# A fused recurrence, tanh feed-forward and top-1 mixture of experts on one core: where the routing's small steps stand in the queues of ScalarE, POOL, SP and PE

## The chip, the cores and the metric

The kernel runs on one core of one Trainium2 chip. The metric is the device time of one execution in microseconds. A profiled execution additionally gives the span from the first to the last instruction and a record of every instruction on the five engines and the DMA queues.

## The reference

Three stages follow one another: a linear recurrence with per-head decay (4 batches, 8 heads, 768 steps, head size 48), a feed-forward layer with `h - tanh(h)`, and a mixture of 8 experts in which each token goes to the one expert with the largest cosine similarity.

```python
# stage 1, per step t
cur = einsum('bhd,bhe->bhde', u[None] * kt, vt)
y[:, :, t] = einsum('bhd,bhde->bhe', rt, state + cur)
state = w[None, :, :, None] * state + einsum('bhd,bhe->bhde', kt, vt)
# stage 2, x is [3072, 384]
h = x @ w_in                     # [384, 2048]
x = (h - np.tanh(h)) @ w_out     # [2048, 384]
# stage 3
xn = x / (norm(x) + 1e-06);  en = expert_emb / (norm(expert_emb) + 1e-06)
logits = xn @ en.T / tau
expert_idx = np.argmax(logits, axis=1)
probs = exp(logits - max);  probs /= probs.sum(-1) + 1e-09
gate_w = probs[arange(N), expert_idx]
for e in range(8):
    out[expert_idx == e] = gate_w * (maximum(x @ w1[e], 0) @ w2[e])   # 384 -> 1024 -> 384
```

## The kernel before, in words

The 3072 tokens are worked in 8 blocks of 3 tiles of 128 tokens. Every product of float32 numbers is made of three products on PE: both operands are split into a rounded half (`hi`) and a remainder (`lo`), and hi·hi, hi·lo, lo·hi are summed in PSUM.

**A block's feed-forward** has 16 steps. A step is `ffn1` (L529 to L536): nine products of 128x384 into one PSUM bank `ph`; then `squares` and `small_tanh` (L574, L583), which make the values on ScalarE (`z` L581, `q` L582, `ghi` L592, a mask L594) and VectorE (L590, L591, `glo` L597); and, three steps later, `ffn2` (L541): nine products that add the step to three accumulators `acc`, one per token tile. The recurrence of the next block is spread between the steps (`pa`, `py`, `am`, L407 to L446). The first six steps of block 0 and the sixteen of block 1 run first, then the other ten of block 0, then blocks 2 to 7, so block 1 is the first to be finished and block 7 the last.

**After a block**, `finish` (L617 to L687) is a generator in four pieces, taken up one at a time. Piece 1 stores the block's rows `xr` to the DRAM table `xs`, takes the logits `l` and the sums of squares `ssq`. Piece 2 finds each token's expert as a one-hot `oh` on VectorE and counts tokens with nine small products on PE into `pk` (L649 to L654). Piece 3 makes each token's row number `irow` on VectorE and lets POOL scatter the token numbers into the DRAM table `tab`, in three indirect DMAs (L666). Piece 4 makes the gate: a root on POOL (`rn`, L673), some small VectorE operations, the exponential `ex` on ScalarE (L678), its sum `se`, and three stores of the gate `gw` by SP into the last columns of `xs` (L686).

**The experts** come after the last block, each with up to 3 tiles of 128 tokens and, for the first ones, a smaller further tile. `places` (L771) loads a list `gts` of token numbers from `tab`, and `rows` (L779) gathers the rows named there from `xs` by indirect DMAs on POOL (L759). The gathered tiles are `rkv` (three per expert), `ktab` and `u_bc`. `columns` (L828) turns a tile on PE (`pt`, L833) and copies it on ScalarE and VectorE to `xt` or `xn`. `load_expert` (L791) loads an expert's weights in four pieces of 768 KB through two staging tiles `eraw` (SP, L799 and L802), each split by ScalarE and VectorE (L810, L811). `wide` (L844) runs the three tiles through 8 steps of `ffn1` (PE L534), `relu` (L610) and `ffn2`; `narrow` (L897) runs a single tile in another arrangement (L904, `hh` L907, L910).

The first expert is chosen while the last block is still computing, so its weights, lists and three tiles are there when the block ends, and its steps 0 to 6 follow at once. What cannot be known before the last block's counts is its fourth tile (`ktab`), and the second expert's list and tiles (`rkv` three times, `u_bc`). At the end of the program's block loop, in this order:

```python
    while pend:
        ffn2_next()
    next(fin)
    next(fin)
    places(0, TB, TB + 1)
    places(1, 0, TB + (KOV > 1))
    for _ in fin:
        pass
    order_rest()
```

What sets the order of work on each engine is a scheduler: the program is written once, the scheduler simulates it with a timeline of its own and puts each engine's instructions into a fixed queue. `with tc.issue_after(x)` adds that what stands inside is placed after the instruction `x`. On the chip every queue is run strictly in order, and an instruction that waits holds up all behind it.

Of the kernel before, what the change touches and what calls it, by code (L numbers as in the profile page):

```python
# [8 lines left out]
F32 = mybir.dt.float32  # L9
# [4 lines left out]
AF = mybir.ActivationFunctionType  # L14
ALU = mybir.AluOpType
# [14 lines left out]
def rwkv__then__tanh_ffn__then__top1_moe_kernel(  # L30
# [14 lines left out]
    nc = tc.nc  # L45
    B = 4
    H, D = w.shape
    NT, DM = out.shape
# [3 lines left out]
    P = 128  # L52
# [475 lines left out]
    def ffn1(lhs, rhs, nk, n, idle=0):  # L528

        ph = ps.tile([P, n], F32, tag="p", name="ph")  # L530
        fill(ph, idle)
        for kk in range(nk):
            for p, (a, b) in enumerate(((0, 0), (0, 1), (1, 0))):
                nc.tensor.matmul(out=ph, lhsT=lhs[a][:, kk, :], rhs=rhs(b, kk),  # L534
                                 start=(kk == 0 and p == 0), stop=(kk == nk - 1 and p == 2))
        return ph  # L536

    def columns_of(xt):
# [46 lines left out]
    def small_tanh(ph, parts, step, between=iter(())):  # L585

        z, q = parts
        ghi = work.tile([P, TOK], F32R, name="ghi", bufs=LAG + 1)
        glo = work.tile([P, TOK], F32R, name="glo", bufs=LAG + 1)
        nc.vector.tensor_tensor(out=ph, in0=ph, in1=z, op=ALU.mult)  # L590
        nc.vector.scalar_tensor_tensor(out=ph, in0=q, scalar=KC, in1=ph, op0=ALU.add, op1=ALU.mult)  # L591
        nc.scalar.activation(out=ghi, in_=ph, func=AF.Copy)  # L592
        mk = work.tile([P, TOK], BF16, name="mk", bufs=1)
        nc.scalar.activation(out=mk, in_=z, func=AF.Relu, bias=lz_t, accum_out=zx[:, step:step + 1])  # L594
        for _ in range(3):
            next(between, None)
        mark["glo"] = nc.vector.tensor_tensor(out=glo, in0=ph, in1=ghi.bitcast(F32), op=ALU.subtract).ins  # L597
        return ghi, glo
# [17 lines left out]
    def finish(j, acc, part=None):  # L616
        l = work.tile([P, TB, E], F32, name="l")  # L617
        ssq = work.tile([P, TB], F32, name="ssq")
        gw = work.tile([P, TB, 2], F32, name="gw")
        for t in range(TB):  # L620
            if part is not None:
                x = part[:, t, :]
                nc.vector.tensor_tensor(out=x, in0=acc[t], in1=x, op=ALU.add)
                acc[t] = x
            nc.vector.tensor_scalar(out=l[:, t, :], in0=acc[t][:, DM:], scalar1=rtau, scalar2=None, op0=ALU.mult)
        for t in range(TB):
            if part is not None:
                xr = part[:, t, :DM]
            else:
                xr = work.tile([P, DM], F32, name="xr")  # L630
                nc.scalar.activation(out=xr, in_=acc[t][:, :DM], func=AF.Copy)
            n = TB * j + t
            nc.sync.dma_start(out=xs[n * P:n * P + P, :DM], in_=xr)
            junk = work.tile([P, TOK], F32, name="t", bufs=1)
            nc.scalar.activation(out=junk, in_=xr, func=AF.Square, accum_out=ssq[:, t:t + 1])
        yield
        bc = [P, TB, E]
        mx = work.tile([P, TB], F32, name="mx")
        nc.vector.tensor_reduce(out=mx, in_=l, op=ALU.max, axis=AX.X)
        nc.vector.tensor_tensor(out=l, in0=l, in1=mx[:, :, None].to_broadcast(bc), op=ALU.subtract)  # L640
        ix = work.tile(bc, F32, name="ix")
        nc.vector.scalar_tensor_tensor(out=ix, in0=l, scalar=0.0, in1=iom[:, None, :].to_broadcast(bc),
                                       op0=ALU.is_ge, op1=ALU.mult)
        nc.vector.tensor_reduce(out=mx, in_=ix, op=ALU.min, axis=AX.X)
        oh = work.tile(bc, BF16, name="oh")
        nc.vector.tensor_tensor(out=oh, in0=iom[:, None, :].to_broadcast(bc),
                                in1=mx[:, :, None].to_broadcast(bc), op=ALU.is_equal)
        pk = ps.tile([P, TB + 1, E], F32, tag="p", name="pk")
        nc.tensor.matmul(out=pk[:, 0, :], lhsT=tri16, rhs=oh[:, 0, :], start=True, stop=True)  # L649
        for t in range(1, TB + 1):  # L650
            if t < TB:
                nc.tensor.matmul(out=pk[:, t, :], lhsT=tri16, rhs=oh[:, t, :], start=True, stop=False)
            for s in range(t):
                nc.tensor.matmul(out=pk[:, t, :], lhsT=ones16, rhs=oh[:, s, :],  # L654
                                 start=(t == TB and s == 0), stop=(s == t - 1))
        yield
        pos = work.tile(bc, F32, name="pos")
        nc.vector.tensor_tensor(out=pos, in0=pk[:, 0:TB, :], in1=cntb[:, None, :].to_broadcast(bc), op=ALU.add)
        nc.vector.tensor_tensor(out=pos, in0=pos, in1=oh, op=ALU.mult)
        row = work.tile([P, TB], F32, name="row")  # L660
        nc.vector.tensor_reduce(out=row, in_=pos, op=ALU.add, axis=AX.X)
        irow = work.tile([P, TB], I32, name="irow")
        nc.vector.tensor_copy(out=irow, in_=row)
        nc.vector.tensor_tensor(out=cntb, in0=cntb, in1=pk[:, TB, :], op=ALU.add)
        for t in range(TB):
            apart("tab", nc.gpsimd.indirect_dma_start(  # L666
                out=tab, out_offset=bass.IndirectOffsetOnAxis(ap=irow[:, t:t + 1], axis=0),
                in_=tokid[:, TB * j + t, :], in_offset=None))
        yield

        rn = work.tile([P, TB], F32, name="rn")
        nc.vector.tensor_scalar(out=rn, in0=ssq, scalar1=1e-30, scalar2=None, op0=ALU.max)
        nc.gpsimd.tensor_tensor(out=rn, in0=rn, in1=half, op=ALU.pow)  # L673
        nc.vector.tensor_scalar(out=rn, in0=rn, scalar1=1e-6, scalar2=None, op0=ALU.add)
        nc.vector.reciprocal(out=rn, in_=rn)
        nc.vector.tensor_tensor(out=l, in0=l, in1=rn[:, :, None].to_broadcast(bc), op=ALU.mult)
        ex = work.tile(bc, F32, name="ex")
        nc.scalar.activation(out=ex, in_=l, func=AF.Exp)  # L678
        se = work.tile([P, TB], F32, name="se")
        nc.vector.tensor_reduce(out=se, in_=ex, op=ALU.add, axis=AX.X)  # L680
        nc.vector.tensor_scalar(out=se, in0=se, scalar1=1e-9, scalar2=None, op0=ALU.add)
        nc.vector.reciprocal(out=se, in_=se)
        nc.vector.tensor_copy(out=gw, in_=se[:, :, None].to_broadcast([P, TB, 2]))
        for t in range(TB):
            n = TB * j + t
            nc.sync.dma_start(out=xs[n * P:n * P + P, DM:], in_=gw[:, t, :])  # L686
        yield  # L687


# [80 lines left out]

    def places(jb, t0, t1):  # L771

        with tc.issue_after(lastg) if jb > 1 else ExitStack():
            eng = nc.gpsimd if jb > 1 else nc.sync
            row = eng.value_load(sxi[0:1, jb, 0:1], min_val=0, max_val=(E - 1) * REG)
            eng.dma_start(out=gts[:, jb, t0:t1],
                          in_=tab[bass.ds(row + t0 * P, (t1 - t0) * P), :].rearrange("(t p) b -> p t b", p=P))

    def rows(jb, t0, t1, n):  # L779
        nonlocal lastg  # L780
# [8 lines left out]
    def load_expert(jb, m, gate, engs=(nc.vector,)):  # L789
# [5 lines left out]
        n = WN // 4  # L795
        for c in range(4):
            t = work.tile([P, n], F32, name="eraw", tag=f"stg{c % 2}", bufs=1)
            if c < 2:
                nc.sync.dma_start(out=t.rearrange("p (k f) -> p k f", k=NK),  # L799
                                  in_=w1e[:, c * 512:(c + 1) * 512].rearrange("(k p) f -> p k f", p=P))  # L800
            else:
                nc.sync.dma_start(out=t.rearrange("p (f d) -> p f d", d=DM),  # L802
                                  in_=w2e.rearrange("(f p) d -> p f d", p=P)[:, 4 * (c - 2):4 * (c - 2) + 4, :])
            m = n // 2
            for s in range(2):
                a = slice(s * m, (s + 1) * m)
                with ExitStack() as es:
                    for g in gate.values():
                        es.enter_context(tc.issue_after(g))
                    nc.scalar.activation(out=hi[c][:, a], in_=t[:, a], func=AF.Copy)  # L810
                    engs[s % len(engs)].tensor_tensor(out=lo[c][:, a], in0=t[:, a], in1=hi[c][:, a].bitcast(F32),  # L811
                                                      op=ALU.subtract)
            yield
# [578 lines left out]
            pass  # L1392
    while pend:
        ffn2_next()
    next(fin)
    next(fin)
    places(0, TB, TB + 1)
    places(1, 0, TB + (KOV > 1))
    for _ in fin:
        pass  # L1400
    order_rest()

    sl = sl + rows(0, TB, TB + 1, NT)
# [73 lines left out]
```

## Time and profile before

| | |
|---|---|
| time, 3 runs | 811.16, 812.74, 815.42 us, median 812.74 us |
| profiled execution | 813.03 us, span 811.4 us |
| PE busy | 778.0 us, 96% of the span, 5938 products |
| VectorE, ScalarE, POOL busy | 506.7, 452.0, 284.1 us |
| mean granted clock of PE | 0.98 |

The granted clock is a share of full speed: 1.00 is 2.4 GHz and 0.50 is 1.2 GHz. A matmul's duration runs to its modelled end, so consecutive ones overlap: nine products of 128x384 take about 1.74 us by their rows. In a timeline, "[4.66 <-DVE l L676]" says that the engine was idle for 4.66 us before the row, until VectorE's instruction of line 676 wrote `l`. Times are microseconds from the span's start.

### The profile page before, as it was taken

The numbers are of one execution on the slowest core, as the hardware profiler recorded it, in microseconds if no ns is written. First come the engines' busy times: TensorE is split into PE (matmuls) and PEld (weight loads), VectorE is DVE, ScalarE is ACT, GpSimd is POOL, SyncE is SP. The second block draws the span as 40 slices with busy tenths as digits, with TensorE's granted clock in tenths as the row PEclk, the third lists the DMA queues.
The fourth block names the chain that finished last, engine by engine and source line by source line (L and its number), as shares of the span: only waits on it lengthen the run. The fifth ranks groups of instructions, "written<-read, shape, count | busy, mean of one in ns | idle before, by whom it ended". The sixth has DMA issues, their size and how long they took to land. (4 is left out here: it accounts for less than half of the span.)

```text
span 811.4 us, 15572 instructions
## 1 busy us (share of the span) xinstructions
PE 778.0 (96%) x5938; PEld 729.3 (90%) x5938; DVE 506.7 (62%) x1080; ACT 452.0 (56%) x1044; POOL 284.1 (35%) x296
## 2 busy tenths in 40 slices
PE   8899999999999999999999999999899999999992
PEld 5679898889999999999999999999789999999992
DVE  7977974766765866875865865686544435554510
ACT  5676686547456556566566567684443444454421
POOL 3721640563550750750741610333340313331111
PEclk9899999999999999999999999999999999999997
DMA  8834350223330240331231210331733445554300
GB/s 275 284 89 134 111 194 1 85 83 122 106 114 23 67 155 21 83 125 43 86 116 54 86 45 15 120 96 31 229 102 118 137 129 166 175 171 143 111 28 30
DMA packets 41861, 87.33 MB, mean 108 GB/s; under 512 B 9744, under 2 KB 21440, under 8 KB 40754
## 3 DMA queue, kind: packets, MB, share of 16 engines
q1 hardware_dynamic: 37042, 76.74, 29.1%
q0 software_dynamic: 4320, 9.51, 3.6%
q8 instruction: 48, 0.79, 0.4%
q14 instruction: 35, 0.29, 0.2%
q10 hardware_dynamic: 416, 0.00, 0.0%
HBM read 67.46 MB, written 19.47 MB: 107 GB/s over the span
## 5 line engine op out<-in xcount | busy, mean ns | idle before, releaser
L534 PE MATMUL ph<-xt,wq 128*128 128x384 f32 (+2 forms) x1712 | 343.4, 343 | 2.2 <-ACT wt L284 1.4
L534 PEld LDWEIGHTS ph<-xt,wq 128*128 128x128 f32 x1712 | 304.2, 190 | 7.8 <-issue 1.7
L545 PE MATMUL acc<-wq,ghi 128*128 128x392 f32 (+2 forms) x1120 | 289.9, 344 | 0.9 <-ACT ghi L610 0.5
L545 PEld LDWEIGHTS acc<-wq,ghi 128*128 128x128 f32 (+1 forms) x1120 | 200.8, 187 | 6.5 <-issue 1.2
L545 PE MATMUL acc<-wq,glo 128*128 128x392 f32 (+2 forms) x560 | 185.6, 342 | 0.0
L581 ACT ACTIVATE z<-ph 128x384 f32<-128x384 f32 x128 | 62.6, 489 | 89.1 <-PE ph L534 88.6
L545 PEld LDWEIGHTS acc<-wq,glo 128*128 128x128 f32 (+1 forms) x560 | 104.3, 187 | 1.3 <-DVE glo L597 0.3
L592 ACT ACTIVATE ghi<-ph 128x384 fp32r<-128x384 f32 x128 | 62.7, 490 | 67.7 <-DVE ph L591 62.9
L590 DVE TENSOR_TENSOR ph<-ph,z 128x384 f32<-128x384 f32 x128 | 71.8, 561 | 45.2 <-ACT z L581 44.8
L597 DVE TENSOR_TENSOR glo<-ph,ghi 128x384 fp32r<-128x384 f32 x128 | 70.9, 554 | 40.9 <-ACT ghi L592 39.7
L764 POOL DMA_INDIRECT out_dram<-ob,gts x27 | 28.7, 1063 | 156.2 <-ACT ob L842 150.7
L582 ACT ACTIVATE q<-z,sb_t 128x384 f32<-128x384 f32 x128 | 78.9, 617 | 3.7
L591 DVE SCALAR_TENSOR_TENSOR ph<-q,ph 128x384 f32<-128x384 f32 x128 | 71.7, 560 | 12.0 <-ACT q L582 3.3
L611 DVE SCALAR_TENSOR_TENSOR glo<-ph,ghi 128x384 fp32r<-128x384 f32 (+2 forms) x56 | 31.4, 563 | 75.5 <-ACT ghi L610 59.8
L594 ACT ACTIVATE mk<-z,lz_t 128x384 bf16<-128x384 f32 x128 | 77.1, 602 | 0.0
L610 ACT ACTIVATE ghi<-ph 128x384 fp32r<-128x384 f32 (+2 forms) x56 | 27.7, 496 | 73.6 <-PE ph L534 72.5
L811 DVE TENSOR_TENSOR wq<-eraw,wq 128x768 fp32r<-128x768 f32 x60 | 58.2, 1008 | 16.0 <-ACT wq L810 11.9
L810 ACT ACTIVATE wq<-eraw 128x768 fp32r<-128x768 f32 x64 | 50.5, 838 | 10.4 <-DMA eraw<-in_moe_w_dram 10.3
L267 POOL TENSOR_TENSOR wq<-wraw,wq 128x768 fp32r<-128x768 f32 (+1 forms) x17 | 30.8, 1810 | 62.6 <-ACT wq L266 62.6
L380 POOL TENSOR_TENSOR rk<-rkv 128x384 f32<-128x384 f32 x18 | 18.4, 1020 | 90.2 <-DMA xs<-xr 42.4
L395 POOL TENSOR_TENSOR am<-ident,cd 128x512 f32<-128x512 f32 x36 | 37.3, 1059 | 11.2 <-DVE cd L385 10.5
L346 POOL TENSOR_TENSOR tt<-tt,tab_k 112x512 f32<-112x512 f32 x20 | 33.2, 1660 | 21.8 <-DMA tt<-in_cols_dram 20.6
(282 smaller groups left out, 886.8 us busy)
## 6 DMA issues: line engine op xcount, KB each, us to landing
eraw<-in_moe_w_dram SPq DMA_DIRECT2D x32, 768.0 KB, 4.9
rkv<-in_rows_dram SPq DMA_DIRECT2D x18, 640.0 KB
tt<-in_cols_dram SPq DMA_DIRECT2D x22, 448.0 KB, 4.0
xd<-xt SPq DMA_DIRECT2D x8, 1152.0 KB, 8.4
wraw<-in_moe_w_in_dram SPq DMA_DIRECT2D x8, 768.0 KB
wraw<-in_moe_w_out_dram SPq DMA_DIRECT2D x8, 768.0 KB, 7.1
xs<-xr SPq DMA_DIRECT2D x21, 192.0 KB, 2.1
rkv<-in_rows_dram SPq DMA_DIRECT2D x4, 256.0 KB, 10.4
```

The lines of the kernel that those rows point to most:

```text
L395: nc.gpsimd.tensor_tensor(out=a, in0=ident[:, None, :].to_broadcast([P, HP, P]), in1=self.cd[:, :, g:g + 1].to_broadcast([P, HP, P]), op=A ...
L534: nc.tensor.matmul(out=ph, lhsT=lhs[a][:, kk, :], rhs=rhs(b, kk), start=(kk == 0 and p == 0), stop=(kk == nk - 1 and p == 2))
L545: mm = nc.tensor.matmul(out=acc[t], lhsT=g[a][:, t * P:t * P + m], rhs=rhs(b, i), start=(i == span[0] and p == 0), stop=(i == span[1] - 1 ...
L581: nc.scalar.activation(out=z, in_=ph, func=AF.Square)
L582: nc.scalar.activation(out=q, in_=z, func=AF.Square, scale=SS, bias=sb_t)
L590: nc.vector.tensor_tensor(out=ph, in0=ph, in1=z, op=ALU.mult)
L591: nc.vector.scalar_tensor_tensor(out=ph, in0=q, scalar=KC, in1=ph, op0=ALU.add, op1=ALU.mult)
L592: nc.scalar.activation(out=ghi, in_=ph, func=AF.Copy)
L594: nc.scalar.activation(out=mk, in_=z, func=AF.Relu, bias=lz_t, accum_out=zx[:, step:step + 1])
L597: mark["glo"] = nc.vector.tensor_tensor(out=glo, in0=ph, in1=ghi.bitcast(F32), op=ALU.subtract).ins
L810: nc.scalar.activation(out=hi[c][:, a], in_=t[:, a], func=AF.Copy)
L811: engs[s % len(engs)].tensor_tensor(out=lo[c][:, a], in0=t[:, a], in1=hi[c][:, a].bitcast(F32), op=ALU.subtract)
```

## The change

Four edits. First, `small_tanh` notes its `ghi` in `mark`, and in all blocks but the last the exponential is placed after the most recent one. Second, in the last block the root moves from piece 4 to piece 3, between the first and the second of POOL's three scatters. Third, at the program's end all of `finish` is taken up before `places`, the places of the first two experts are placed after the last gate's store, and the second expert's weights after its list. Fourth, in the last block the counts are placed after the last product of `ffn1`.

```diff
@@ ffn1
-                nc.tensor.matmul(out=ph, lhsT=lhs[a][:, kk, :], rhs=rhs(b, kk),
-                                 start=(kk == 0 and p == 0), stop=(kk == nk - 1 and p == 2))
+                mark["ph"] = nc.tensor.matmul(out=ph, lhsT=lhs[a][:, kk, :], rhs=rhs(b, kk),
+                                              start=(kk == 0 and p == 0), stop=(kk == nk - 1 and p == 2)).ins
@@ small_tanh
-        nc.scalar.activation(out=ghi, in_=ph, func=AF.Copy)
+        mark["ghi"] = nc.scalar.activation(out=ghi, in_=ph, func=AF.Copy).ins
@@ finish
-        nc.tensor.matmul(out=pk[:, 0, :], lhsT=tri16, rhs=oh[:, 0, :], start=True, stop=True)
+        with tc.issue_after(mark["ph"]) if j == NB - 1 else ExitStack():
+            nc.tensor.matmul(out=pk[:, 0, :], lhsT=tri16, rhs=oh[:, 0, :], start=True, stop=True)
...
+        rn = work.tile([P, TB], F32, name="rn")
+        def norms():
+            nc.vector.tensor_scalar(out=rn, in0=ssq, scalar1=1e-30, scalar2=None, op0=ALU.max)
+            return nc.gpsimd.tensor_tensor(out=rn, in0=rn, in1=half, op=ALU.pow).ins
+        root = None
         for t in range(TB):
-            apart("tab", nc.gpsimd.indirect_dma_start(
-                out=tab, out_offset=bass.IndirectOffsetOnAxis(ap=irow[:, t:t + 1], axis=0),
-                in_=tokid[:, TB * j + t, :], in_offset=None))
+            with tc.issue_after(root) if root else ExitStack():
+                apart("tab", nc.gpsimd.indirect_dma_start(
+                    out=tab, out_offset=bass.IndirectOffsetOnAxis(ap=irow[:, t:t + 1], axis=0),
+                    in_=tokid[:, TB * j + t, :], in_offset=None))
+            if j == NB - 1 and t == 0:
+                root = norms()
         yield
-        rn = work.tile([P, TB], F32, name="rn")
-        nc.vector.tensor_scalar(out=rn, in0=ssq, scalar1=1e-30, scalar2=None, op0=ALU.max)
-        nc.gpsimd.tensor_tensor(out=rn, in0=rn, in1=half, op=ALU.pow)
+        if j < NB - 1:
+            norms()
...
-        nc.scalar.activation(out=ex, in_=l, func=AF.Exp)
+        with tc.issue_after(mark["ghi"]) if j < NB - 1 else ExitStack():
+            nc.scalar.activation(out=ex, in_=l, func=AF.Exp)
...
-            nc.sync.dma_start(out=xs[n * P:n * P + P, DM:], in_=gw[:, t, :])
+            mark["gw"] = nc.sync.dma_start(out=xs[n * P:n * P + P, DM:], in_=gw[:, t, :]).ins
@@ places
-        with tc.issue_after(lastg) if jb > 1 else ExitStack():
+        with tc.issue_after(lastg) if jb > 1 else tc.issue_after(mark["gw"]):
...
-            eng.dma_start(out=gts[:, jb, t0:t1],
+            mark["gts"] = eng.dma_start(out=gts[:, jb, t0:t1], in_=tab[bass.ds(row + t0 * P, (t1 - t0) * P), :]
...
@@ load_expert, around the loads of a piece
+            with tc.issue_after(mark["gts"]) if jb == 1 else ExitStack():
...
@@ the end of the block loop
-    next(fin)
-    next(fin)
+    for _ in fin:
+        pass
     places(0, TB, TB + 1)
     places(1, 0, TB + (KOV > 1))
-    for _ in fin:
-        pass
     order_rest()
```

Since the scheduler writes the queues, three places of them are shown, before and now. The lines of the changed program are higher by up to 16.

The first is ScalarE's queue where block 1 is finished, among the steps of block 0: `z`, `q`, `mk` and `ghi` are one step's values. Before:

```order
L592 ACTIVATE ghi<-ph 128x384
L678 ACTIVATE ex<-l 128x24
L581 ACTIVATE z<-ph 128x384
L582 ACTIVATE q<-z,sb_t 128x384
L594 ACTIVATE mk,zx<-z,lz_t 128x384
```

And with the change:

```order
L592 ACTIVATE ghi<-ph 128x384
L581 ACTIVATE z<-ph 128x384
L582 ACTIVATE q<-z,sb_t 128x384
L594 ACTIVATE mk,zx<-z,lz_t 128x384
L592 ACTIVATE ghi<-ph 128x384
...
L592 ACTIVATE ghi<-ph 128x384
L692 ACTIVATE ex<-l 128x24
```

The exponential, which stood ahead of the next step's values, now stands behind those of two steps. In the later blocks it moves behind one or two `ghi`; in the last block it stood behind the `ghi` (L610) of the first expert's step 3 and now stands ahead of it.

The second is SP's queue at the end of the last block: `xr` and `gw` are stores into `xs`, `gts` the loads of the two lists, `eraw` the second expert's weights; a TENSOR_LOAD reads a number from memory into a register of SP. Before:

```order
L633 DMA xs<-xr 128x384 x3
L791 TENSOR_LOAD sxi
L791 ISA x2
L776 ISA
L776 DMA gts<-tab 128x2
L776 ISA
L776 DMA gts<-tab 128x4x2
L799 ISA
L799 DMA eraw<-in_moe_w_dram 128x3x512
...
L686 DMA xs<-gw 128x2 x3
```

And with the change:

```order
L633 DMA xs<-xr 128x384 x3
...
L700 DMA xs<-gw 128x2 x3
L789 TENSOR_LOAD sxi
L789 ISA x2
L790 ISA
L790 DMA gts<-tab 128x2
L789 TENSOR_LOAD sxi
...
L790 DMA gts<-tab 128x4x2
L815 ISA
L815 DMA eraw<-in_moe_w_dram 128x3x512
```

The three stores of gates moved from behind the lists and two pieces of weights to ahead of them, and a register is now read between the stores and the first list and between the lists.

The third is PE's queue in the first expert: `acc_7109` to `acc_7111` are its three accumulators, `wq_1378` and `wq_1379` the halves of the last weights, and `pt` the turned tiles that hang on the gathers. Before:

```order
L545 MATMUL acc_7109<-wq_1378,glo 128x384
L545 MATMUL acc_7110<-wq_1378,glo 128x384
L545 MATMUL acc_7111<-wq_1378,glo 128x384
L833 MATMUL pt<-ident,ktab 128x128 x3
L833 MATMUL pt<-ident,rkv_119 128x128 x9
L833 MATMUL pt<-ident,u_bc 128x64 x3
L534 MATMUL ph<-xt,wq_72 128x384 x2
```

And with the change:

```order
L545 MATMUL acc_7111<-wq_1378,glo 128x384
L849 MATMUL pt<-ident,ktab 128x128 x3
L545 MATMUL acc_7109<-wq_1378,ghi 128x384
...
L545 MATMUL acc_7109<-wq_1379,ghi 128x384
L849 MATMUL pt<-ident,rkv_119 128x128 x3
L545 MATMUL acc_7110<-wq_1378,ghi 128x384
L849 MATMUL pt<-ident,rkv_119 128x128 x3
```

The scheduler has moved the turned tiles forward: `ktab`'s now stands behind step 4 of `ffn2`, and those of the second expert among the products of step 6; before, all stood behind step 6. The nine counts (`pk`) stand in the same place of PE's queue as before: behind `ffn1` of the first expert's step 0 and the last block's last products, ahead of the first expert's step 1.

## Rows read from the trace of the kernel before

**Rows 1.** Waits of PE over the span: for what; us in total, times, longest
```profile
PE py L438 <- DVE am L412: 2.6, 1, 2.6
PE pt L833 <- DMA rkv<-xs,gts: 1.9, 1, 1.9
...
PE pk L649 <- DVE oh L646: 1.5, 1, 1.5
...
PE pt L833 <- DMA ktab<-xs,gts: 1.0, 1, 1.0
PE pt L910 <- issue: 0.7, 1, 0.7
...
PE acc L545 <- ACT ghi L610: 0.5, 1, 0.5
```

**Rows 2.** Windows: us, busy of PE, PEld, DVE, ACT, POOL; granted clock, DMA share, GB/s
```profile
164.00:168.00 4.00, 4.00 (x15) 3.73 (x14) 2.10 (x5) 1.97 (x5) 2.05 (x4) 0.58 0.09 3
585.00:589.00 4.00, 3.65 (x14) 3.22 (x13) 1.68 (x7) 0.82 (x2) 0.00 (x0) 0.50 0.36 133
589.00:594.00 5.00, 5.00 (x22) 4.33 (x21) 2.39 (x3) 2.86 (x5) 0.00 (x0) 0.77 0.13 15
```

**Rows 3.** Timeline of ScalarE, block 1's finish: start us, us, engine, line, operation, idle before
```profile
161.46 0.22 ACT L678 ACTIVATE ex<-l 128x24 f32<-128x24 f32 x1 [4.66 <-DVE l L676]
```

**Rows 4.** Timeline of VectorE, block 1's finish
```profile
160.33 1.10 DVE L676 TENSOR_TENSOR l<-l,rn 128x24 f32<-128x24 f32 x1
...
162.10 0.57 DVE L590 TENSOR_TENSOR ph<-ph,z 128x384 f32<-128x384 f32 x1
...
162.66 0.70 DVE L412 COPY_PREDICATED am<-cmask,pa 128x512 f32<-128x512 uint8 x1
```

**Rows 5.** Timeline of PE, last block and first expert
```profile
542.28 1.15 PE L833 MATMUL pt<-ident,rkv 128*128 128x128 f32 x9
...
572.45 1.74 PE L534 MATMUL ph<-xt,wq 128*128 128x384 f32 x9
...
586.17 3.25 PE L534 MATMUL ph<-xt,wq 128*128 128x384 f32 x9
```

**Rows 6.** Timeline of SP's DMA queue, last block and first expert
```profile
520.21 0.42 SPq L776 DMA_DIRECT2D gts<-tab  x1
...
565.76 0.94 SPq L776 DMA_DIRECT2D gts<-tab  x2
566.97 1.02 SPq L799 DMA_DIRECT2D eraw<-in_moe_w_dram  x2
569.20 1.35 SPq L686 DMA_DIRECT2D xs<-gw  x3
574.93 2.48 SPq L802 DMA_DIRECT2D eraw<-in_moe_w_dram  x2
```

**Rows 7.** Timeline of POOL, last block and first expert
```profile
523.96 1.06 POOL L759 DMA_INDIRECT rkv<-xs,gts  x1 [6.69 <-issue]
...
562.14 0.96 POOL L666 DMA_INDIRECT tab<-tokid,irow  x1 [0.30 <-issue]
563.13 0.92 POOL L673 TENSOR_TENSOR rn<-rn,half 128x3 f32<-128x3 f32 x1
...
575.74 1.33 POOL L759 DMA_INDIRECT ktab<-xs,gts  x1 [11.32 <-issue]
...
581.35 1.00 POOL L759 DMA_INDIRECT u_bc<-xs,gts  x1 [0.31 <-issue]
```

**Rows 8.** Line L686 alone, all 24 stores of gates: the row on landing
```profile
DMA to landing us min/median/max: 1.4/1.5/5.2
```

**Rows 9.** Timeline of ScalarE, first expert
```profile
574.27 1.59 ACT L810 ACTIVATE wq<-eraw 128x768 fp32r<-128x768 f32 x2 [0.49 <-DMA eraw<-in_moe_w_dram]
...
579.66 1.58 ACT L810 ACTIVATE wq<-eraw 128x768 fp32r<-128x768 f32 x2 [3.04 <-DMA eraw<-in_moe_w_dram]
```

**Rows 10.** Timeline of VectorE, last block
```profile
566.52 0.16 DVE L683 COPY gw<-se 128x6 f32<-128x6 f32 x1
```

More of the change, by code (lines that the diff above doesn't have):

```diff
@@ L771, in places @@
     def places(jb, t0, t1):
-        with tc.issue_after(lastg) if jb > 1 else ExitStack():
+        with tc.issue_after(lastg) if jb > 1 else tc.issue_after(mark["gw"]):
             eng = nc.gpsimd if jb > 1 else nc.sync
             row = eng.value_load(sxi[0:1, jb, 0:1], min_val=0, max_val=(E - 1) * REG)
-            eng.dma_start(out=gts[:, jb, t0:t1],
-                          in_=tab[bass.ds(row + t0 * P, (t1 - t0) * P), :].rearrange("(t p) b -> p t b", p=P))
+            mark["gts"] = eng.dma_start(out=gts[:, jb, t0:t1], in_=tab[bass.ds(row + t0 * P, (t1 - t0) * P), :]
+                                        .rearrange("(t p) b -> p t b", p=P)).ins
     def rows(jb, t0, t1, n):
@@ L797, in load_expert @@
             t = work.tile([P, n], F32, name="eraw", tag=f"stg{c % 2}", bufs=1)
[L798 to L803, printed above, removed]
+            with tc.issue_after(mark["gts"]) if jb == 1 else ExitStack():
+                if c < 2:
+                    nc.sync.dma_start(out=t.rearrange("p (k f) -> p k f", k=NK),
+                                      in_=w1e[:, c * 512:(c + 1) * 512].rearrange("(k p) f -> p k f", p=P))
+                else:
+                    nc.sync.dma_start(out=t.rearrange("p (f d) -> p f d", d=DM),
+                                      in_=w2e.rearrange("(f p) d -> p f d", p=P)[:, 4 * (c - 2):4 * (c - 2) + 4, :])
             m = n // 2
```

## The prediction

> **What bounds the kernel now.** PE does nearly all of the span, so I read its waits first. Apart from the start-up there are two places where it waits for something that the change touches. One wait of 2.6 us, for VectorE's `am`, is where block 1 is finished. The others lie together at the first expert: 0.5 for a `ghi`, 1.0 for the gathered `ktab`, 1.9 for the gathered `rkv`, 0.7 in the fourth tile's path, 4.1 us in all; 1.5 us for `oh` stands a little ahead of them [rows 1]. Second, the windows: behind both places PE's granted clock is low, 0.58 over 164 to 168 and 0.50 and 0.77 over 585 to 589 and 589 to 594 [rows 2]. Low is the level of 1.2 GHz, and each time it came behind PE's idle time. One step's nine products took 1.74 us ahead of it and 3.25 in it [rows 5]. Third, the queues, for what ended the waits.
>
> At the first expert the chain goes back to one order in SP's queue. The second expert's weights were issued at 566.97, the gates' stores behind them at 569.20 [rows 6]. A store of gates takes a median of 1.5 us to land, the slowest 5.2 [rows 8]. POOL's first gather waited 11.32 us and started at 575.74, the last of the five ended at 582.35 [rows 7]: that fits stores held up behind 1.5 MB on the same queue, which the gathers need because they read the gate's columns.
>
> **The change part by part.**
>
> *The exponential behind `ghi`.* Where block 1 is finished ScalarE sat 4.66 us before `ex` with the next step's `z` behind it [rows 3]. Now `z` goes first. What is late next is VectorE: its `l` ends at 160.33 + 1.10 = 161.43, and the step's product (L590) and then `am`'s copy follow in its queue. The product ran at 162.10 and the copy at 162.66 [rows 4], 0.56 apart, so the copy can start at about 161.95, 0.7 sooner, and with the two small gate steps gone from between them perhaps 0.8. The bounds are 0 (VectorE meets POOL's transfers anyway) and all of the 2.6 us with its low clock, (1 - 0.58) x 4.0 = 1.7, so 4.3. I take 0.8, because VectorE's own chain is in the rows and stays; the idle time of some 2 us left is nearer to the 2.6 that brought the clock down than to nothing.
>
> In blocks 0 and 2 to 6 no wait of PE hangs on `ex`: 0. The gates there are stored one or two steps later; only the gathers read them. The nearest is block 6, ahead of the first expert's gathers at 523.96 [rows 7], whose tiles PE turns at 542.28 [rows 5]. A delay of two steps is some 6 us against 18; if that cover were gone, PE would wait for the rest. VectorE's `se` now waits for `ex` directly behind a `ghi`, for which `glo` waits too: 0.
>
> *The counts behind nine products.* In PE's queue they stand where they stood, because the last `ffn1` before them was already ahead. The 1.5 us for `oh` stays, and what is behind it (step 1's products) waits as before: 0.
>
> *The root between the scatters.* On POOL the root (0.92 us) goes ahead of two scatters of 0.96 and their 0.3 us gaps [rows 7]: it comes 2.5 us sooner, and the last scatter ends some 1.0 us later, at 564.1. The gate was ready at 566.68 [rows 10], 2.6 us behind the root's end. Now the root ends near 561.5 and the gate comes at 564 to 565, with `ex` no longer behind a `ghi` that waits for step 3.
>
> *SP's queue.* Three stores of gates take 1.35 us to issue [rows 6], until 566.4 at the latest, and land 1.5 later, by 568. The lists wait for the scatters: the first went out at 565.76, 2.7 us behind the last scatter's end [rows 6, 7], so now at 566.8. Behind them the weights: a register read costs about 0.6 us (two lie in the 1.2 us between 567.99 and 569.20), so the weights go out at 568.0 to 568.3 instead of 566.97, 1.2 us later.
>
> *The gathers.* In the last block the first gather started 3.75 us behind the list's issue (520.21 to 523.96) [rows 6, 7]. From 566.8 that gives 570.5. The five took 6.6 us, so the last is issued by 577.1, 5.2 us sooner than before. `ktab` was turned by PE at 580.86 [rows 5], 3.8 us behind its gather's end at 577.07. So it lands at 575.6, the others 1.3 us apart until 580.4.
>
> By the Trainium skill ("DMA: Bandwidth & Descriptors", Anatomy of one DMA) a POOL transfer takes about 2.0 us plus its bytes over 436 GB/s, here an estimate of 2.5 us for the 198 KB of 128 rows. The row's 3.8 is beside two pieces of weights and decides; by the page's figure the gathers land 1.3 us sooner and the time would be about 806.
>
> *PE.* Step 6's nine products began at 572.45 and took 1.74 [rows 5]; step 4's nine of `ffn2` behind them take as long, so PE reaches `ktab`'s tile at about 575.9, and with the products now between the tiles the last one at about 580.2. The gathers are there just in time. Step 5's `ghi` stands ahead of the weights' copies now, so its 0.5 goes. Not all goes: the weights' second pair is issued when the first pair's copies are done, so it too is 1 to 2 us later. Its first copy waited 3.04 us for a transfer issued 4.7 us before [rows 6, 9], and behind it on ScalarE stand the last tiles, step 7's `ghi` and, behind the other copy, `hh`. I leave 1.5 us of waits for that. With 1.5 us in pieces, as at `oh` where the next products ran at full clock, the clock should stay up. The low clock cost 3.65 x 0.50 + 5.00 x 0.23 = 3.0 us [rows 2]. So this place gives 4.1 + 3.0 - 1.5 = 5.6. The bounds are 0 (the waits only move) and 7.1. From there on PE is the bound, and the gain stays to the end.
>
> The sum, against the profiled execution's 813.03 us (span 811.4 and 1.6 around it; 0.3 above the median of the three runs): 813.0 - 0.8 - 5.6 = **806.6 us**.
>
> **The rivals.**
>
> *The gathers come no sooner than the weights (0.21).* The first pair was issued at 566.97 and its second copy began at 574.27, having waited for it [rows 6, 9]: 7.3 us. From 568.0 that is 575.3, and the gathers' traffic comes on top. If each gather is signalled only when what was issued before it has landed, `ktab` comes at 577.5 or later and the last tile at 582. For it speaks that a transfer on SP's own queue was held up so. Against it, POOL's transfers have a queue of their own. PE then waits 1.6 us at once, with steps 5 and 6 behind the tile that used to cover it, 0.8 more at the last tiles and the 1.5 above: 3.9, nearly what it was, and the clock falls as before. Only block 1's 0.8 stays, and perhaps half a microsecond: about **811.8**.
>
> By the Trainium skill (same page, Queues, rings and completion order) a transfer's semaphore is written only after every earlier write of that DMA engine, across its queues. No run here shows it so far; `ktab`'s 3.8 us beside weights is more than the same page's 2.5 and would fit.
>
> *All of it goes (0.14).* The copies come in time, and block 1's idle time is now too short to bring the clock down: 813.0 - 0.8 - 1.7 - 7.1 = **803.4**.
>
> *The clock stays low through the first expert (0.07, slower).* The mechanism is the tiles standing among the products: several short waits from 576 on instead of three together at 581 to 584, and the clock falls early and comes back only when the fourth tile's path is over, near 600. Each microsecond of work at the low level costs half a microsecond. The stretch now cost 3.0; with the 2.6 of waits and 0.8 of block 1 saved, the gain is gone at 6.4 us of loss, some 13 us at the low level, and at 21 us it is 4 us slower: **817**. For it speaks that both idle places of 2.6 us and more were followed by a low clock; against it that `oh`'s 1.5 us was not.
>
> **How the numbers follow.** The forecast has 0.58, with a range of its own of 804.5 to 809. A measurement of this kernel can tell 0.5% (4.1 us) from no change. Faster by more takes the third case and nine tenths of the forecast: 0.66. Within it lie the rest of the forecast and the first rival: 0.27. Slower: 0.07. The range of 803.4 to 812.2 leaves out the slower case and the ends of the others, about 0.15.
>
> **What would show it.** Right: the last block's stores of gates landing in about 1.5 us; the first gather starting at 570 to 571 and the last at 576; `ktab` and `rkv` gone from PE's waits or under 1 us; clock 1.00 from 575 to 600; the second expert's first products some 5 to 6 us earlier in the span; 1.5 us for `oh` unchanged; at block 1 a wait of 1.8 to 2.0 for `am`. Wrong: a first gather later than 573; a wait of PE for weights' copies, `xn` or `hh` of over 2 us; a stretch of low clock over 6 us at the first expert; or a new wait in blocks 2 to 6 or at the first expert's tiles.

## The result, and the profile after

The changed kernel took 802.72 us (median of 17 runs, 800.26 to 810.43) against 810.3 us of the kernel before on the same chips (17 runs, 807.95 to 815.42): a ratio of 0.9895, 95% interval 0.9878 to 0.9912, or 8.5 us less by the ratio (the two medians are 7.6 us apart). Timed again later it came to 0.9873 (0.9853 to 0.9894). The forecast was 806.6 from 813.0, 6.4 us less. The time lies 0.7 us below the range's low end of 803.4. The profiled execution took 802.88 us (span 801.3, clock 0.987).

PE's waits after the change, the answers to [rows 1] (for what; us in total, times, longest):

```profile
PE pk L651 <- DVE oh L646: 1.5, 1, 1.5
PE py L438 <- DVE am L412: 0.9, 1, 0.9
PE pt L926 <- ACT hh L923: 0.9, 2, 0.7
...
PE acc L545 <- DVE glo L611: 0.3, 1, 0.3
```

`ktab`, `rkv`, `u_bc` and `ghi` are gone from the list, `am` is down from 2.6 to 0.9 and `oh` stands at 1.5 as before. The windows of [rows 2], in the same columns:

```profile
164.00:168.00 4.00, 4.00 (x60) 3.54 (x59) 1.45 (x3) 1.71 (x4) 3.01 (x4) 1.00 0.16 12
585.00:589.00 4.00, 3.31 (x19) 2.78 (x18) 3.31 (x9) 1.39 (x3) 3.08 (x4) 1.00 0.93 297
589.00:594.00 5.00, 5.00 (x29) 4.63 (x28) 1.55 (x8) 0.55 (x1) 2.24 (x3) 1.00 0.49 157
```

The clock, 0.58, 0.50 and 0.77 before, is 1.00 in all three. SP's DMA queue and POOL at the last block, against [rows 6, 7]:

```profile
560.82 1.28 SPq L700 DMA_DIRECT2D xs<-gw  x3
562.95 1.52 SPq L790 DMA_DIRECT2D gts<-tab  x2
564.72 1.01 SPq L815 DMA_DIRECT2D eraw<-in_moe_w_dram  x2
572.67 2.97 SPq L818 DMA_DIRECT2D eraw<-in_moe_w_dram  x2
```

```profile
556.94 0.88 POOL L671 TENSOR_TENSOR rn<-rn,half 128x3 f32<-128x3 f32 x1
...
565.85 1.05 POOL L773 DMA_INDIRECT ktab<-xs,gts  x1 [5.07 <-DMA gts<-tab]
...
571.15 1.46 POOL L773 DMA_INDIRECT u_bc<-xs,gts  x1 [0.30 <-issue]
```

The stores now go out first, then the lists, then the weights. Three marks on PE show where the time went: block 6's counts, block 7's counts, and the product at the end of the first expert. Before:

```profile
512.03 0.18 PE L649 MATMUL pk<-oh,tri 128*128 128x8 bf16 x1
...
557.98 0.18 PE L649 MATMUL pk<-oh,tri 128*128 128x8 bf16 x1 [1.46 <-DVE oh L646]
...
599.81 0.18 PE L982 MATMUL pok<-ok,ones 128*128 128x8 bf16 x1
```

And with the change:

```profile
509.45 0.18 PE L651 MATMUL pk<-oh,tri 128*128 128x8 bf16 x1
...
554.24 0.18 PE L651 MATMUL pk<-oh,tri 128*128 128x8 bf16 x1 [1.47 <-DVE oh L646]
...
589.37 0.18 PE L998 MATMUL pok<-ok,ones 128*128 128x8 bf16 x1
```

At block 6's counts the changed kernel is 2.58 us ahead (block 1's place). Block 7 took 44.79 us instead of 45.95: 1.16 more. The first expert took 35.13 instead of 41.83: 6.70 more. Together that is 10.4 us, in two single executions; the ratio of all runs is worth 8.5. Behind the third mark the two kernels took the same time to the span's end, 211.6 and 211.9 us, so the gain stayed to the end as forecast.

### The profile page after: what moved, and what is told of

Same layout as the page of the kernel before. It is cut to its first block, busy times and chain, and to the rows that moved or that the text cites. A ratio compares the mean times of both kernels' runs of the same rounds, so it can differ in the third digit from the quotient of the medians.

```text
span 801.3 us, 15575 instructions
## 1 busy us (share of the span) xinstructions
PE 772.8 (96%) x5938; PEld 726.3 (91%) x5938; DVE 506.8 (63%) x1080; ACT 451.5 (56%) x1044; POOL 283.9 (35%) x296
## 5 line engine op out<-in xcount | busy, mean ns | idle before, releaser
L590 DVE TENSOR_TENSOR ph<-ph,z 128x384 f32<-128x384 f32 x128 | 71.9, 561 | 46.3 <-ACT z L581 45.4
L591 DVE SCALAR_TENSOR_TENSOR ph<-q,ph 128x384 f32<-128x384 f32 x128 | 71.8, 561 | 12.5 <-ACT q L582 3.6
L610 ACT ACTIVATE ghi<-ph 128x384 fp32r<-128x384 f32 (+2 forms) x56 | 27.8, 497 | 72.5 <-PE ph L534 66.6
L827 DVE TENSOR_TENSOR wq<-eraw,wq 128x768 fp32r<-128x768 f32 x60 | 55.1, 956 | 12.0 <-ACT wq L826 10.4
L346 POOL TENSOR_TENSOR tt<-tt,tab_k 112x512 f32<-112x512 f32 x20 | 33.1, 1657 | 17.8 <-DMA tt<-in_cols_dram 17.8
```

## The experiments

Ratios are to the kernel before in runs on the same chips, with 95% intervals. The table has all fourteen profiles: PE's wait for `am` at block 1, the clock over 164 to 168, and the time between the three marks. (The waits end between 160.1 and 164.7 us; over the 12 us behind each of them the clock says the same.)

| kernel | ratio | wait for `am` | clock | block 7 | first expert |
|---|---|---|---|---|---|
| before | | 2.65 | 0.58 | 45.95 | 41.83 |
| before, again | 1.0011 | 1.88 | 0.57 | 45.72 | 42.76 |
| no halves on POOL | 1.0003 | 1.85 | 0.64 | 44.79 | 42.86 |
| exponential only | 1.0033 | 0.90 | 1.00 | 51.73 | 40.98 |
| exponential and first fence | 0.9967 | 0.85 | 1.00 | 44.78 | 43.49 |
| weights behind gates | 0.9955 | 1.86 | 1.00 | 45.76 | 38.69 |
| change without exponential | 0.9910 | 1.71 | 0.59 | 46.25 | 34.78 |
| change without root | 0.9891 | 0.85 | 1.00 | 44.79 | 37.15 |
| the change | 0.9895 | 0.90 | 1.00 | 44.79 | 35.13 |
| the change, again | 0.9873 | 0.90 | 1.00 | 44.79 | 37.60 |
| weights early | 0.9862 | 0.88 | 1.00 | 44.79 | 34.36 |
| counts late | 0.9861 | 0.90 | 1.00 | 81.96 in all | |
| both | 0.9852 | 0.90 | 1.00 | 78.60 in all | |
| both, again | 0.9881 | 0.99 | 1.00 | 78.46 in all | |

In the last three the counts of block 7 stand behind nine more products, so only the sum of both stretches can be compared: 79.92 and 82.39 in the two profiles of the change.

**The exponential only**, on the kernel before:

```diff
-        nc.scalar.activation(out=ghi, in_=ph, func=AF.Copy)
+        mark["ghi"] = nc.scalar.activation(out=ghi, in_=ph, func=AF.Copy).ins
...
-        nc.scalar.activation(out=ex, in_=l, func=AF.Exp)
+        with tc.issue_after(mark["ghi"]) if j < NB - 1 else ExitStack():
+            nc.scalar.activation(out=ex, in_=l, func=AF.Exp)
```

> Only the exponential's place is changed (behind the last ghi, all blocks but the last), on the kernel before. Theory A (the three places add up, each for its own cause): block 1's wait for am falls from 2.6 to 1.0 us or less, the clock over the 4 us behind it stays at 1.00, and the time falls by 2.6 us (2.0 to 3.4); at the first expert all is as before, with some 4 us of waits and a stretch of low clock. Rival B (block 1's clock was chance, and only the exponential's 0.8 us as forecast is to be had): a wait of 1.8 to 2.0 us with low clock behind it, and the time falls by 0.8 us or not at all.

It was slower: 1.0033 (1.0013 to 1.0053). Block 1 did what theory A said. The loss is in block 7, which neither theory had. SP's queue, POOL, ScalarE and PE there:

```profile
520.01 0.97 SPq L800 DMA_DIRECT2D eraw<-in_moe_w_dram  x2
521.08 1.51 SPq L687 DMA_DIRECT2D xs<-gw  x3
534.70 2.21 SPq L803 DMA_DIRECT2D eraw<-in_moe_w_dram  x2
```

```profile
528.65 1.52 POOL L760 DMA_INDIRECT rkv<-xs,gts  x1 [12.58 <-DMA xs<-gw]
...
532.83 3.66 POOL L812 TENSOR_TENSOR wq<-eraw,wq 128x768 fp32r<-128x768 f32 x2
```

```profile
539.68 1.58 ACT L811 ACTIVATE wq<-eraw 128x768 fp32r<-128x768 f32 x2 [4.92 <-DMA eraw<-in_moe_w_dram]
```

```profile
544.07 0.55 PE L834 MATMUL pt<-ident,rkv 128*128 128x128 f32 x3 [3.00 <-DVE glo L597]
...
546.32 3.25 PE L534 MATMUL ph<-xt,wq 128*128 128x384 f32 x9 [0.75 <-DVE glo L597]
```

With the exponential later, block 6's stores of gates fell behind the first expert's weights on SP (521.08 behind 520.01), just as the last block's had stood behind the second expert's. The first gather came at 528.65 instead of 523.96 [rows 7]; POOL's split of the weights stood behind the gathers, the next two pieces could be issued only at 534.70, ScalarE waited 4.92 us for them, and PE stood 3.75 us, with nine products at the low clock behind it.

**The exponential and a first fence**: the same, and the first expert's list behind block 6's stores, as the change has it too.

```diff
-                places(0, 0, TB)
+                with tc.issue_after(mark["gw"]):
+                    places(0, 0, TB)
```

> The kernel before with the exponential moved in all blocks but the last (as in the run that was slower with this alone) and one thing more: the first expert's list, and with it its weights behind it on SP, are placed behind block 6's stores of gates. Theory A (that run lost its time because block 6's stores stood behind the first expert's weights): the stores land in 2 us instead of 5 to 6, the first gather of block 7 starts near 523 to 524 instead of 528.7, the waits for glo (3.7 us) and the low clock behind them go, and the time is 1 to 3 us below the kernel before (block 1 and block 7 as in the changed kernel, the second expert's place as before). Rival (the exponential's own place makes ScalarE or VectorE late in block 7): waits of 2 us or more in block 7 stay and the time is at or above the kernel before.

0.9967 (0.9951 to 0.9983), 2.7 us less: theory A. SP's queue and POOL:

```profile
517.68 1.29 SPq L687 DMA_DIRECT2D xs<-gw  x3
...
520.43 0.97 SPq L800 DMA_DIRECT2D eraw<-in_moe_w_dram  x2
```

```profile
522.84 1.06 POOL L760 DMA_INDIRECT rkv<-xs,gts  x1 [8.66 <-issue]
```

So the exponential's move was worth its time only together with the third edit, whose fence also covers the first expert's list.

**The change without the exponential** (`with tc.issue_after(mark["ghi"]) ...` taken away again):

> The changed kernel with the exponential left free as before; root, stores of gates, lists and weights as changed. Theory A: block 1 again shows a wait for am of about 2.6 us and a clock near 0.6 behind it; the first expert keeps its gain of 6.7 us; against the kernel before the time falls by 6 to 7 us, so it lies 2 to 3 us above the changed kernel. Rival B: the time is within 1 us of the changed kernel's.

0.9910 (0.9881 to 0.9939), 7.3 us less. Block 1 showed 1.71 us and a clock of 0.59 and block 7 took 46.25, as in the kernel before; the first expert's 34.78 is the change's. Against the change the difference is 0.0015 or 1.2 us, less than the intervals, and between theory A's 2 to 3 us and rival B's 1 us: this run decides between neither.

**The change without the root**: `norms()` for all blocks stands behind the scatters again.

> The changed kernel with the root behind the three scatters again; the scheduler then puts all turned tiles behind step 6 of the first expert, as before the change. Theory A (what counts is that the stores of gates go out ahead of the weights): the stores go out some 2.5 us later than in the changed kernel, the first gather starts 2 to 2.5 us later (near 568), the last is issued near 574, all land before PE is through with step 6 (near 576), no wait for ktab or rkv over 0.5 us, clock 1.00 but for the fourth tile's path, and the time is 0 to 1.5 us above the changed kernel's. Rival C (what counts is that PE meets the tiles spread among products): with the tiles in one piece again the waits come back at 2 us or more with a low clock behind them, and 3 to 5 us of the gain go.

0.9891 (0.9861 to 0.9920), the change's own time. The stores went out at 563.42, 9.3 us behind block 7's counts instead of 6.6, the tiles stood in one piece for `rkv`, and PE waited 1.35 us for `ktab`, with the clock at 1.00. Rival C fell for those tiles (`ktab` still stood nine products ahead of them), and the second edit brought nothing that can be measured.

**Weights behind gates**, one edit on the kernel before:

```diff
+            with tc.issue_after(mark["gw"]) if jb == 1 else ExitStack():
                 if c < 2:
                     nc.sync.dma_start(...)
```

> The kernel before with one edit: the second expert's weights are placed behind the last block's stores of gates on SP; lists, root and exponential as before. Theory A: the stores, ready at about 566.7, go out by 568.3 and land in 1.5 us instead of up to 5.2; the first gather starts near 570 to 571 instead of 575.7, the waits for ktab and rkv (2.9 us) go, and the time falls by 4 to 6 us; the weights are 1.5 to 2.5 us later, which leaves 1 to 3 us of waits for ghi or hh. Rival D (the gathers are held up by the weights' transfers wherever these stand in the queue, or by their lists): the first gather starts not before 574, and the time falls by 1 us at most.

0.9955 (0.9934 to 0.9976), 3.6 us less. The first gather started at 569.83, behind the counts by 13.9 us instead of 17.8: that order held the stores up, and rival D fell. The gain is below theory A's 4 to 6 us: `ktab` and `rkv` are gone from the waits, but a new one stands there. PE, POOL, SP's queue and ScalarE:

```profile
581.08 0.40 PE L834 MATMUL pt<-ident,u_bc 64*128 64x64 f32 x3 [3.13 <-DMA u_bc<-xs,gts]
```

```profile
575.19 1.50 POOL L759 DMA_INDIRECT u_bc<-xs,gts  x1 [0.30 <-issue]
```

```profile
575.87 2.57 SPq L803 DMA_DIRECT2D eraw<-in_moe_w_dram  x2
```

```profile
580.87 1.58 ACT L811 ACTIVATE wq<-eraw 128x768 fp32r<-128x768 f32 x2 [3.05 <-DMA eraw<-in_moe_w_dram]
```

The last gather ended at 576.69, and weights were issued on SP at 575.87, ahead of its end. PE got the tile at 581.08, when the first piece of those weights too had landed (ScalarE got it at 580.87).

**The kernel before and the change, again**, for second profiles:

> The kernel before, unchanged, for a second profile. If block 1's low clock belongs to its wait for am, the wait of 1.7 to 2.7 us and a clock near 0.6 behind it are there again; if it is chance, the clock may stay at 1.00 behind a wait of the same length, as in the run with the weights behind the gates. The ratio should be 1.000, within 0.002. At the first expert the waits (4 us) and the low clock should be there again, and block 6's counts to block 7's should again take 45.9 us with one subtraction of 4.1 us.

> The changed kernel once more, for a second profile and for a time on the same chip as the next run. The ratio to the kernel before should be 0.9895 within 0.002; at block 1 a wait of 0.8 to 0.9 us and a clock of 1.00 behind it; from the last block's counts to the first expert's end 35 to 36 us, against 41.8 to 43.5 in the profiles without the gates' stores moved; no stretch of low clock between 575 and 600.

The kernel before showed low clock and waits in the same places, so the clock at block 1 is no accident of one profile. But the wait there was 1.88 us instead of 2.65 (`l` took 0.17 us, as in every later profile, and 1.10 only in the one of [rows 4]), and the subtraction expected at 4.1 us took 1.27. The change met its 37.60 instead of 35 to 36 by one wait, in PE, POOL, SP's queue and ScalarE:

```profile
580.00 0.40 PE L849 MATMUL pt<-ident,u_bc 64*128 64x64 f32 x3 [1.89 <-DMA u_bc<-xs,gts]
```

```profile
574.07 1.49 POOL L773 DMA_INDIRECT u_bc<-xs,gts  x1 [0.30 <-issue]
```

```profile
574.75 2.82 SPq L818 DMA_DIRECT2D eraw<-in_moe_w_dram  x2
```

```profile
579.96 1.58 ACT L826 ACTIVATE wq<-eraw 128x768 fp32r<-128x768 f32 x2 [2.33 <-DMA eraw<-in_moe_w_dram]
```

It is the picture of the run with the weights behind the gates: weights issued 0.8 us ahead of the gather's end, and both landed at 580.0. In the change's first profile the weights were issued at 572.67, just behind that gather's end at 572.61, and the tile was there when PE came at 575.76.

**No halves on POOL**, on the kernel before: `load_expert(0, ..., (nc.vector, nc.gpsimd))` loses its last argument.

> The kernel before with the first expert's weights split by VectorE alone instead of by VectorE and POOL in turn. In block 7 one of VectorE's subtractions took 4.11 us instead of 0.96, beside two of POOL's back to back (3.65 us), and PE lost 0.83 us at that step. Theory A (the two engines' subtractions stood in each other's way): all of VectorE's now take 0.96 us, PE's wait of 0.3 us for ghi in block 7 goes, and from block 6's counts to block 7's it takes 44.8 to 45.2 us as in the changed kernel instead of 45.95; the time falls by 0.7 to 1.2 us. Rival (the place of the weights' copies on ScalarE made ghi late): the long subtraction goes but the 45.95 us stay, or grow by the four subtractions that VectorE has now to do more.

Block 7 took 44.79 us, as theory A said; the time did not move, 1.0003 (0.9981 to 1.0024), an interval that holds the 0.9 us. The pair it takes apart, in the kernel before, on VectorE and POOL:

```profile
528.78 4.11 DVE L811 TENSOR_TENSOR wq<-eraw,wq 128x768 fp32r<-128x768 f32 x1
```

```profile
528.41 3.65 POOL L811 TENSOR_TENSOR wq<-eraw,wq 128x768 fp32r<-128x768 f32 x2
```

**Counts late, weights early, both.** Counts late:

```diff
     while pend:
         ffn2_next()
+    with tc.issue_after(mark["acc"]):
+        next(wides[0])
     for _ in fin:
```

(`mark["acc"]` is the last product of `ffn2`; the second expert's loads start one step later in the program.) Weights early: the loads of the second expert's first two pieces are written where the first line added above stands, and `load_expert` takes them up; the fence behind the second expert's list is gone there.

> The changed kernel with its fourth edit made to work: the nine products of the first expert's step 1 are placed behind the last block's last products, and the counts behind them, so that PE has them to do while VectorE makes oh. Theory A: the wait of 1.5 us for oh goes, the counts come no more than 0.3 us later, and the time falls by 1.2 to 1.5 us against the changed kernel (ratio to the kernel before about 0.988). Rival: the routing chain is what ends last there, and with VectorE's and ScalarE's queues lengthened by a step the first list, the gathers and the fourth tile come later by as much: no gain, the time within 0.4 us of the changed kernel's.

> The changed kernel with the second expert's first two pieces of weights issued on SP ahead of the last block's rows, as soon as the staging tiles are free, so that they land before the gates' stores go out; the second two pieces then follow the lists. Theory A (gathers and weights only share bandwidth and order): the stores of gates and the lists come as in the changed kernel, ktab comes no later, the waits for hh and glo (1.2 us) fall by half or more, the time is 0.3 to 1 us below the changed kernel's. Rival (a gather is signalled only with the weights issued just ahead of it, 7.3 us from their issue): the second pair now stands in that place, ktab comes 2 us or more later than in the changed kernel, and PE waits for it: 1 to 3 us above the changed kernel.

> The two last edits together (counts behind step 1's nine products, first two pieces of weights early). Theory A: the gains add: 1.5 to 2.5 us below the changed kernel. Rival as for the early weights: the counts' gain is eaten by later gathers, the time within 1 us of the changed kernel's or above it.

> The version with counts behind step 1's products and the first two pieces of weights early, on the same chip as the changed kernel. If both gains are real and add: 2 to 3.5 us below the changed kernel (ratio to the kernel before 0.985 to 0.987). If they stand in each other's way or were chance: within 1 us of the changed kernel.

On one chip they came to 0.9861 (0.9835 to 0.9887), 0.9862 (0.9834 to 0.9890) and 0.9852 (0.9828 to 0.9876), all below the change's 0.9895, with intervals that overlap or nearly touch its own. The wait for `oh` is gone in both kernels with late counts; in the profile with these alone 2.49 us for `u_bc`, and a low clock, took its place. With early weights the stores of gates came 9.5 us behind block 7's counts instead of 6.6 and the first gather 2.6 us later, and the second pair of weights stood just ahead of it, as the rival had it; but PE met the tiles without a wait. The two stretches took 78.5 us in both profiles of the last version. But beside the change on the same chip it was no faster: both medians were 803.07 us. The 1.3 to 3.9 us that the profiles show at this place are not shown in the time.

## Why the prediction was right or wrong

Two terms of the sum were off: what the exponential's move brings, and the time that the gains were taken from. Either of the two alone is more than the 0.7 us by which the time lies below the range.

**The first expert: right, a little small.** The forecast was 5.6. The two first profiles give 6.70. Over the profiles, the five with the stores behind the weights took 42.4 us on the mean, the four of the change and its variants without exponential or root 36.2: 6.2. The order was as told: stores, lists, weights; the first gather 11.6 us behind block 7's counts (forecast 12.5, before 17.8); `ktab` turned at 572.03 without a wait, and the clock up. How long the last block's stores took to land, the change's trace does not hold; without the root it was 1.4 to 1.5 us, without the exponential 2.3 to 2.6, before 5.2. (The median of 1.5 in [rows 8] is that of the three landings that the trace holds, of 24 stores.) The 1.5 us left for waits came to 1.2 in the first profile (`hh` and `glo`), and in the second to 1.89 for `u_bc`, a wait that brought the clock down.

**The first rival's delay was at work, its price was not.** Its rule was that a gather is signalled only when what was issued before it has landed. In five profiles PE waited for `ktab` where weights had gone out just ahead of its gather (without exponential, without root, counts late, and both profiles of the version with both edits): the tile came 4 to 5.7 us behind the gather's end, and 7.3 to 7.5 us behind the weights' issue. In the two profiles shown above, `u_bc` came with the weights (580.00 and 579.96; 581.08 and 580.87). With the change's weights issued at 564.72, `ktab` would come at about 572.0: that is when it was turned. The DMA queues of the change show the cause (POOL's transfers are on q0, SP's on q1; packets, MB, share of 16 engines). From 565.8, when the first gather was issued, to 570.7:

```profile
q1 hardware_dynamic: 723, 1.45, 96.8%
q0 software_dynamic: 6, 0.00, 0.1%
```

And from 571.6 to 573.7:

```profile
q0 software_dynamic: 194, 0.45, 63.1%
q1 hardware_dynamic: 1, 0.00, 0.0%
```

So the gathers' own bytes, and not their signal alone, came behind the weights, though on another queue. Where no weights were under way, at the first expert with the exponential only, the three gathers landed 3.0 to 3.7 us behind their issue; `ktab` behind weights took 5.5 (weights behind gates) and 6.3 us (without exponential). The Trainium skill ("DMA: Bandwidth & Descriptors", Queues, rings and completion order) has the semaphore written behind every earlier write of the same engine, whatever its queue; no row here speaks against it, and none can show it, since the bytes themselves were late.

The forecast had `ktab` land 3.8 us behind its gather's end; by the 7.3 us it took about 5.1. That cost nothing because the gather had started 0.9 us sooner than forecast and PE came to the tile just then. That part was luck. The rival's 811.8 came from the 2 us and more that I had added for the gathers' own traffic; `ktab`, the first of them, needed no such time. (A slip that decided nothing: tiles 1.3 us apart from 575.6 end at 580.8, not at 580.4.)

**The exponential: the step that failed.** The prediction said 0.8 at block 1 and "In blocks 0 and 2 to 6 no wait of PE hangs on `ex`: 0."
- The wait itself was sized well: 1.71 to 1.88 in the four other profiles without the edit, 0.85 to 0.99 in all nine with it, a difference of 0.9. The 2.65 that I started from held 0.9 us of a slow `l`. So what was left was not "1.8 to 2.0" but 0.9, and the clock behind it stayed at 1.00 nine times of nine; without the edit it fell four times of five. From block 1's counts to the next ones, block 0's, the five took 50.6 us on the mean, the nine 48.2. I had called the rest "nearer to the 2.6" and left the clock's 1.7 us out. That was half of the third case, which I had given 0.14.
- Block 7 got 1.0 us shorter, which no step had: 44.8 in the five profiles with the edit and the fence that can be compared, 45.7 to 46.3 in four of the five without. With the exponential later and the fence, ScalarE's fifth and sixth copies of the first expert's weights ran back to back (from 534.23, 1.58 us for both) and not 2.75 us apart (535.11 and 537.86). That the copies on POOL have a part in the loss is shown by taking them off (44.79 with the exponential in its old place); that it is the long subtraction is not, since with one of 1.27 us the kernel before still took 45.72. How the later exponential takes the loss away stays open.

Block 1's 0.9 and 1.7 and block 7's 1.0 make 3.6 where 0.8 stood; timed with its fence the edit gave 2.7 (1.4 to 4.0), and taken out of the change 1.2, which the intervals tell neither from 2.7 nor from nothing. The danger that the prediction saw for block 6's gathers, a later store, was real as well: alone, the edit made the kernel 2.7 us slower (0.0033 of 812), with the stores behind the weights. I had checked it against a cover of 18 us and not against SP's queue, where the stores moved behind 1.5 MB.

**The counts and the root: right.** `oh` stayed at 1.5; the root moved the stores 2.7 us and the time by nothing.

**The base: the second term that was off.** The forecast was set against a profile at 813.0 and three runs; the median of 17 is 810.3, 2.7 us lower. The ratio put on 813.0 gives 804.5, inside the range; the range in microseconds had no room for the base. The third case's 803.4 was nearest.

## What to carry to other kernels

A small store that gathers wait for should stand in its DMA queue ahead of any large load, for every block: an edit that delays it slightly can put it behind one, so look at the queue's order after the edit and not at the cover in microseconds. A large load issued just ahead of the gathers, though on another queue, also held their bytes up here. A wait of PE that stood alone cost its length and, from 1.7 us on in all cases but one, a stretch at the low clock behind it (1.7 us more at block 1); bringing it well below that can be worth more than the 0.9 us that it gets shorter. And take the wait's length from more than one profile, and the base from more than three runs.

## What the runs showed that was not expected

- **Waits and the clock.** Behind block 1 and later, for waits that stand alone: behind 0.85 to 0.99 us (nine) and 1.46 to 1.47 (eleven, for `oh`) the clock stayed at 1.00; behind 1.71, 1.85 and 1.88 it fell to 0.57 to 0.64, behind 1.86 it did not; behind 1.89, 2.5, 2.65 and 3.1 it fell. So the length alone does not decide. In the start-up this is plainer: behind a wait of 1.57 us, for `ktok`, the clock was 0.50 over 45.4 to 48.4 in the kernel before; behind one of 1.56 it was 1.00 over 46.6 to 49.8 with the exponential and the first fence.
- **VectorE beside POOL.** A subtraction of 128x768 took 4.11 us instead of 0.96 while POOL did two of its own from 528.41 to 532.06; it ended at 532.89, as if it had begun when POOL was done. The Trainium skill ("SBUF — State Buffer", SBUF: two separate sides) says that the two engines share a port pair, which one holds for a whole instruction while the other is blocked, also where VectorE's instruction has two inputs in SBUF and POOL's reads SBUF; the row agrees, though VectorE waited out two instructions of POOL and not one.
- **Most of the spread between these executions** lies early: block 0's counts came between 201.07 and 205.60 us in the nine profiles with the exponential moved, and the program is the same up to there; from there to block 6's counts they took 306.1 to 307.3 us.
